# Staging the float64 words of the fourth weight matrix in two rooms of their own, in a delta-rule attention kernel with two feed-forward blocks

## The chip, the cores and the metric

The kernel runs on one core of one Trainium2 chip. The metric is the time of one execution on the device, in microseconds (us). In what follows PE is TensorE (the matmuls), DVE is VectorE, ACT is ScalarE, POOL is GpSimd and SP is the queue that issues the DMAs.

## What is computed

The reference is a delta-rule attention with a state per head, followed by two feed-forward blocks without a residual. The weights of the blocks come as float64, all else as float32.

```python
for t in range(S):                       # batch 4, 8 heads, S = 768, D = 48
    kt, vt, bt = (k_n[:, :, t], v[:, :, t], beta[:, :, t, None])
    y[:, :, t] = np.einsum('bhd,bhde->bhe', q[:, :, t], state)
    v_old = np.einsum('bhde,bhd->bhe', state, kt)
    state = state + bt[:, :, :, None] * np.einsum('bhd,bhe->bhde', kt, vt - v_old)
x = y.transpose(0, 2, 1, 3).reshape(3072, 384)
h = x @ w1_in;  x = np.maximum(0.01 * h, h) @ w1_out       # 384 -> 2048 -> 384
h = x @ w2_in;  out = (h - np.tanh(h)) @ w2_out            # 384 -> 2048 -> 384
```

## The kernel before

**Tiles.** The sequence is cut into 12 chunks n of 64 steps; two chunks make a unit u (6 units). A chunk carries 256 tokens (4 batches of 64 steps). For each unit the attention prepares keys and queries, Gram matrices, the inverse of a triangular matrix per head (`inverses(u)`, a chain of some sixty small POOL instructions), merges, states and outputs. `outputs(n)` writes the attention result of chunk n; it gathers its operands in two tiles of 128 partitions by 2048 float16, `Ub` and `Sb`, whose off-diagonal blocks must be zero. `to_xa(n)` scales and splits that result into the input of the first block; `to_xb(n)` does the same between the blocks.

**Feed-forward layers.** The last loop of the kernel calls `layer(n, i)` for each unit in the order (2u,0), (2u+1,0), (2u,1), (2u+1,1). A layer is 8 steps p. In each, `h_part` multiplies by the first matrix of block i (18 matmuls of 256 columns) and applies the nonlinearity, and three steps later (`LAG` is 3) `o_part` multiplies by the second matrix. All matmuls are made from float16 high and low halves.

**Weights.** The four matrices w1_in, w1_out, w2_in, w2_out are here called weights 0 to 3; each stands in 16 slices. `weights()` takes them one after the other. For each, `Weights.load` issues one DMA of 384 KB per slice, from float64 words into a *room* of 768 32-bit words per partition, as long as no room is asked for that still holds words not yet used. `convert` turns two slices at a time into float32 by three DVE instructions on the words (`w_f32`), sums their squares on ACT (the squares themselves are thrown away into the room), and then calls `load` again. Where the two rooms of a pair lie side by side in one tile the pair is one set of three instructions, 768 results wide; otherwise it is two sets of 384. After the eight pairs a matrix-wide scale is worked out (`sw`), and a second generator, `splits`, makes the float16 high half (two ACT instructions) and the low half (one on DVE or POOL) of each slice. `need((2 * i + 1, 2 * p + 1))` in `o_next` holds `o_part` back until the slices of its step are split.

The rooms of weights 3 are four of the eight slots of the tile that the matrix itself will fill (each used twice, for slices 0 to 7), and the first 768 words of `Ub` and of `Sb` (each used four times, for slices 8 to 15). So `weights()` waits for `("y", 1)`, the end of `outputs(1)`, before it touches weights 3, zeroes both tiles on POOL behind the conversion, and `outputs(n)` with n > 1 waits for `"w2"`, which stands for that.

**What sets the order.** The instructions are not ordered by hand. Every piece of work is a Python generator that yields the time from which it could go on, by a simple cost model kept in `Plan`. `Side.first` takes the generator with the smallest of that time plus a fixed delay for its kind (`d_...`); `Side.step`, called between matmuls of the layers, runs what is due; `Side.fill` puts pieces of `weights()` into gaps that the model sees on DVE; `need` and `layer` force work when the layers can't go on without it. The result is one fixed sequence per engine, and each engine runs its own in order. The delays and some other settings come from `START` until `"w2"` is done, then from `STEADY` (`tune`). Of the delays, smaller goes first: in `START` d_s2 is -1, d_w 0, d_s3 0.5, d_s1 1.0 and d_q (queries) 4.4; in `STEADY` d_q is 3.4, d_xa -1 in place of 0, and `step` is called after every second matmul of a layer, not every third.

Every instruction is issued in one helper, line 160, so the profile shows that line everywhere and the tiles tell what is what: `h_ps` and `o` are the sums of the layers, `a_ps` those of the attention and of the scales; `wo` and `wi` are weight tiles, `wst` the scaled slice, `wacc` the sums of squares; `X` and `Gd` the inverse; `sx`, `g`, `kap` and `osb` belong to the layers.

Of the kernel before, what the change touches and what calls it, by code (L numbers as in the profile page):

```python
# [7 lines left out]
F32 = mybir.dt.float32  # L8
# [183 lines left out]
def kernel(  # L192
# [13 lines left out]
    pe, act, dve, pool, sp = (Engine(plan, n) for n in ("pe", "act", "dve", "pool", "sp"))  # L206
# [8 lines left out]
    NF = w1_in.shape[1] // (KT * 128)  # L215
    DM = KT * 128
# [10 lines left out]
    def room(name, bufs, **kw):  # L227
        return Room(plan, ctx.enter_context(tc.tile_pool(name=name, bufs=bufs, **kw)), bufs)

    const, wts, live = (room(n, 1) for n in ("const", "wts", "live"))  # L230
# [16 lines left out]
    def copy(o, i, scale=1.0):  # L247
        act.activation(out=o, in_=i, func=ACTF.Copy, scale=scale)
# [16 lines left out]
    def cp(o, i, scale=None):  # L265

        op = "tensor_copy" if scale is None else "tensor_scalar"
        fa, fd = plan.finish("act", "activation", [i], [o]), plan.finish("dve", op, [i], [o])
        ca, cd = plan.cost("act", "activation", [o, i]), plan.cost("dve", op, [o, i])
        if fa + tune("cp") * (ca - cd) < fd:  # L270
            copy(o, i, 1.0 if scale is None else scale)
        elif scale is None:
            dve.tensor_copy(out=o, in_=i)
        else:
            dve.tensor_scalar(out=o, in0=i, scalar1=scale, scalar2=None, op0=ALU.mult)
# [74 lines left out]
    WO = [wts.tile([128, NF, 2, DM], F16, name=f"wo{i}") for i in range(2)]  # L350
    WI2 = [w.rearrange("p f c t n -> p f c (t n)") for w in WI]
    sw = const.tile([128, 6], F32, name="sw")

    def words(t):

        t = t.bitcast(I32)
        n = DM * 2
        return [t[:, i * n:(i + 1) * n] for i in range(t.shape[1] // n)]
# [64 lines left out]
    def weights():  # L423
        wi = [words(w.rearrange("p f c n -> p (f c n)")) for w in WI2]
        wo = [words(w.rearrange("p f c n -> p (f c n)")) for w in WO]
        nh = len(wi[0])

        x = [words(x_tile("w1"))[0] for _ in range(2)]
        a = Weights(0, w1_in, WI2[0], wo[0] + wo[1])
        b = Weights(1, w1_out, WO[0], ((wi[1] + x) * 2)[0:NF])  # L430
        yield Part([], 0)
        yield from a.convert()
        side.add(a.splits(), "s0")
        a = Weights(2, w2_in, WI2[1], (wo[1] * 2)[0:NF])
        yield from b.convert()
        side.add(b.splits(), "s1")
        done.add("w1")
        yield from a.convert()
        side.add(a.splits(), "s2")
        yield from wait(("y", 1))  # L440
        yield Part([], 0)
        bs = [words(t.rearrange("p c m n -> p (c m n)"))[0] for t in (Ub, Sb)]
        r = wo[1][nh // 2:] * 2 + bs * (NF // 4)
        b = Weights(3, w2_out, WO[1], r)
        yield from b.convert()
        for t in (Ub, Sb):
            pool.memset(t, 0.0)
        done.add("w2")
        side.add(b.splits(), "s3")

# [10 lines left out]
    Ub = live.tile([128, 2, GM, 128], F16, name="Ub")  # L461
    Sb = live.tile([128, 2, GM, 128], F16, name="Sb")
# [4 lines left out]
    def bank(n):  # L467
        t = ps_a.tile([128, 512], F32, tag="a", name="a_ps")
        return t[:, 0:GM * n].rearrange("p (m n) -> p m n", m=GM)

    def mm3(o, lb, ls, rhs, start=True, stop=True):
        mm(o, lb[:, 0, ls], rhs[0], start, False)
        mm(o, lb[:, 0, ls], rhs[1], False, False)
        mm(o, lb[:, 1, ls], rhs[0], False, stop)

    def halves(dst, src, n, w, rows=None):
        for h in range(2):
            r = (rows or HS)[h]
            cp(dst[r, :, :, w * h:w * h + n], src[r])
# [21 lines left out]
    def x_tile(owner):  # L501

        x_owner.append(owner)
        return x_p.tile([128, KT * N], F32, tag="x", name="x")
# [3 lines left out]
    def wait(key):  # L508
        if key not in done:
            yield lambda: key in done  # L510
# [371 lines left out]
    def outputs(n):  # L882
        u, s = n // 2, n % 2
        yield from wait(("u", n))
        yield from wait(("pp", n))
        yield from wait(("x", u))
        Q, P = q_t.pop(n), p_t.pop(n)
        if n > 1:
            yield from wait("w2")
            yield from wait(("r", n - 3))  # L890
            yield from wait(x_owner[-NX])
            x_t[n] = x_tile(("a", n))
        x32 = x_t[n].rearrange("p (t b i) -> p t b i", t=KT, b=B)

        def fill_y(g):
            halves(Ub, R[:, g], D, D)
            if n > 0:
                halves(Sb, SP[:, :, g * GM:(g + 1) * GM], D, D, HD)

        for g in range(NG):  # L900
            qs = qs_t[n, g]
            dve.tensor_scalar(out=qs[:, 4:5], in0=qs[:, 3:4], scalar1=sv_t[u, s][:, 3:4], scalar2=KS, op0=ALU.mult,
                              op1=ALU.mult)
        fill_y(0)
        for g in range(NG):
            yield Part([Ub, Sb, P[:, g]], 1)
            ps = bank(C)
            for m in range(GM):
                if n > 0:
                    mm3(ps[:, m], Sb, m, (Q[:, g, 0, m], Q[:, g, 1, m]), stop=False)  # L910
                mm3(ps[:, m], Ub, m, (P[:, g, 0, m], P[:, g, 1, m]), start=n == 0)
            if g + 1 < NG:
                fill_y(g + 1)
                done.add(("f", n))
            pv = ps.rearrange("p (b t) i -> p t b i", t=HP)
            xv = x32[:, :, g * 2:g * 2 + 2]
            sc = qs_t.pop((n, g))
            copy(xv[0:96], pv[0:96, 0:KT], sc[0:96, 4:5])
            for t_ in range(KT):
                cp(xv[96:128, t_], pv[32 * t_:32 * t_ + 32, KT], sc[32 * t_:32 * t_ + 32, 4:5])  # L920
        done.add(("y", n))
        side.add(to_xa(n), "xa")
# [25 lines left out]
    def to_xa(n):  # L948

        x = x_t.pop(n)  # L950
        yield max(plan.t["act"], at(x))
        sx = sm_p.tile([128, 4], F32, tag="sxs", name="sxs", bufs=4)
        pow2_scale(sx[:, 0:1], (yield from squares(x)), XT)
        yield at(sx[:, 0:1])
        xa_t[n] = x_split(x, sx[:, 0:1]), sx
        done.add(("n", n))
# [143 lines left out]
    def all_outputs():  # L1100
        for n in range(NS):
            yield from outputs(n)
# [60 lines left out]
    with tc.manual_schedule():  # L1163
# [18 lines left out]
        for gen, d in ((first_keys(), "k0"), (v_scale(0, 0), "v"), (all_outputs(), "o"), (all_states(), "s"),  # L1182
                       (all_products(), "p"), (all_merges(), "m"), (all_inverses(), "i"),
                       (all_grams(range(2)), "g0"), (all_queries(), "q"), (all_grams(range(2, 2 * NU)), "g"),
                       (all_keys(), "k")):
            side.add(gen, d)
        side.add(weights(), "w", True)
        plan.filler = side.fill
        for u in range(NU):
# [50 lines left out]
```

## Time and profile before

| | |
|---|---|
| median of 3 runs | 1244.53 us (1243.42 to 1246.35) |
| the profiled execution's own time | 1241.99 us |
| its span in the trace | 1240.3 us |
| PE busy in the span | 1012.0 us (82%) |
| DVE, ACT, POOL busy | 727.6, 635.0, 512.9 us |
| mean granted clock of PE | 0.959 of 2.4 GHz |

The durations below come from the profiled execution. Its time is 1.69 us above its span and 2.54 us below the median of the runs. Times of day in the text are us from the start of the span. A PE that is shown busy may still be running at the lower of its two clocks.

### The profile page before, as it was taken

To read this page: it belongs to the slowest core of one execution; us is meant where nothing else is said; L and a number is where in the kernel's file an instruction comes from. 1 tells how busy PE (TensorE), PEld (TensorE's weight loads), DVE (VectorE), ACT (ScalarE), POOL (GpSimd) and SP (SyncE) were. 2 spreads that over 40 slices of the span, in tenths; PEclk is the share of its full clock that TensorE was granted. 3 is DMA by queue.
4 is the path that set the end of the run, shared out by engine and by line. 5 is a ranking of instruction groups with operands and counts; after the bars stand their busy time and mean duration, and the time that the engine had idled before them with its cause. 6 is when DMAs were issued, how large, how long until landed. Compare 5 with 4: busy or idle time off the path is not lost.

```text
span 1240.3 us, 36912 instructions
## 1 busy us (share of the span) xinstructions
PE 1012.0 (82%) x16216; PEld 832.3 (67%) x16216; DVE 727.6 (59%) x1609; ACT 635.0 (51%) x1414; POOL 512.9 (41%) x635
## 2 busy tenths in 40 slices
PE   0202679682876999989998899979999999999998
PEld 0202568571765788867687786768867888778875
DVE  7998844886768756776566577326654154420243
ACT  3556687746475555745455655325543354333342
POOL 4697365398238624771177304831210221012100
PEclk9999999895788999989999999989999999999999
DMA  9423010421000101000101000001000000000001
GB/s 359 160 72 112 3 28 18 164 60 39 16 25 23 45 16 46 23 23 3 27 15 37 12 24 10 14 14 32 25 10 14 14 11 2 1 17 11 1 1 26
DMA packets 21857, 48.17 MB, mean 39 GB/s; under 512 B 4288, under 2 KB 7360, under 8 KB 21696
## 3 DMA queue, kind: packets, MB, share of 16 engines
q1 hardware_dynamic: 21696, 45.82, 11.8%
q8 instruction: 126, 2.06, 0.7%
q14 instruction: 35, 0.29, 0.1%
HBM read 41.09 MB, written 4.72 MB: 37 GB/s over the span
## 4 chain that ended last, share of the span: by engine, by line
PE 54%; DVE 22%; ACT 13%; POOL 6%; issue 4%; DMA 1%; SPq 0%; ACTq 0%; POOLq 0%; DVEq 0%
PE o L160 22%; PE h_ps L160 21%; PE a_ps L160 10%; POOL X L160 2%; DVE n L160 2%; DVE wi L160 2%; DVE wo L160 2%; DVE x L160 2%; DVE sx L160 2%; ACT g L160 2%; POOL Gd L160 2%; ACT junk L160 2%; DVE g L160 2%; ACT sx L160 1%; DVE Ub L160 1%
## 5 line engine op out<-in xcount | busy, mean ns | idle before, releaser
L160 PE MATMUL h_ps<-x,wi 128*128 128x256 f16 x3456 | 422.5, 275 | 18.7 <-DVE x L160 6.3
L160 PEld LDWEIGHTS <-wi 128*128 128x128 f16 x3456 | 334.2, 98 | 76.5 <-issue 15.8
L160 PE MATMUL o<-wo,g 128*128 128x384 f16 x1152 | 213.2, 334 | 22.3 <-ACT wo L160 7.4
L160 POOL TENSOR_TENSOR g<-sx,g 128x512 f16<-128x512 f32 x80 | 96.2, 1203 | 314.5 <-ACT g L160 305.3
L160 PE MATMUL o<-g,wo 128*128 128x256 f16 x1728 | 211.0, 275 | 0.0
L160 PEld LDWEIGHTS <-wo 128*128 128x128 f16 x1728 | 167.2, 98 | 31.5 <-issue 9.3
L160 ACT ACTIVATE g<-sx 128x512 f16<-128x512 f32 x192 | 121.0, 630 | 119.5 <-DVE sx L160 116.5
L160 PEld LDWEIGHTS <-g 128*128 128x128 f16 x1152 | 112.5, 99 | 88.1 <-issue 27.1
L160 DVE SCALAR_TENSOR_TENSOR sx<-sx,kap,h_ps 128x512 f32<-128x512 f32 x96 | 71.2, 742 | 98.5 <-ACT sx L160 98.3
L160 POOL TENSOR_TENSOR X<-X,Gd 128x30 f32<-128x30 f32 (+9 forms) x180 | 116.1, 645 | 14.1
L160 POOL TENSOR_TENSOR Gd<-X 128x30 f32<-128x30 f32 (+9 forms) x180 | 108.4, 602 | 27.6 <-DVE X L160 15.2
L160 ACT ACTIVATE sx<-h_ps,kap 128x512 f32<-128x512 f32 x96 | 65.5, 683 | 92.2 <-PE h_ps L160 86.5
L160 ACT ACTIVATE sx<-h_ps 128x512 f32<-128x512 f32 x96 | 56.6, 590 | 105.5 <-PE h_ps L160 101.5
L160 DVE SCALAR_TENSOR_TENSOR g<-sx,g 128x512 f16<-128x512 f32 x96 | 71.4, 743 | 64.7 <-ACT g L160 64.6
L160 PEld LDWEIGHTS <-KTp 64*64 64x64 f16 x3360 | 66.4, 119 | 36.0 <-issue 34.5
L160 PE MATMUL a_ps<-ab,ones 128*128 128x1 bf16 x124 | 11.4, 168 | 95.7 <-DVE ab L160 93.7
L160 POOL TENSOR_TENSOR P<-P,maskp 128x1024 f16<-128x1024 f16 x24 | 54.7, 2288 | 67.9 <-DVE P L160 66.4
L160 PEld LDWEIGHTS <-KN 64*64 64x64 f16 x1824 | 39.1, 123 | 43.4 <-issue 39.1
L160 PEld LDWEIGHTS <-ones 128*128 128x128 bf16 x124 | 7.7, 103 | 79.9 <-DVE ab L160 51.5
L160 DVE COPY Ub<-R 64x768 f16<-64x768 f16 x47 | 23.4, 498 | 56.6 <-PE a_ps L160 56.1
L160 PE MATMUL a_ps<-Q,KTp 64*64 64x64 f16 x1152 | 24.6, 199 | 23.3 <-ACT Q L160 20.2
L160 PE MATMUL a_ps<-Q,Sb 128*128 128x64 f16 x528 | 36.7, 201 | 8.4 <-DVE Sb L160 8.4
(165 smaller groups left out, 1538.8 us busy)
## 6 DMA issues: line engine op xcount, KB each, us to landing
wo<-in_w_in_dram SPq DMA_DIRECT2D x32, 384.0 KB, 6.5
qf<-in_q_dram SPq DMA_DIRECT2D x24, 256.0 KB, 3.1
wi<-in_w_out_dram SPq DMA_DIRECT2D x14, 384.0 KB, 7.8
kf<-in_k_dram SPq DMA_DIRECT2D x12, 384.0 KB, 3.8
vf<-in_v_dram SPq DMA_DIRECT2D x12, 384.0 KB, 3.6
out_dram<-osb SPq DMA_DIRECT2D x48, 96.0 KB, 2.2
wo<-in_w_out_dram SPq DMA_DIRECT2D x8, 384.0 KB, 5.4
Ub<-in_w_out_dram SPq DMA_DIRECT2D x4, 384.0 KB, 3.3
```

The source lines that it names most:

```text
L160: return getattr(self.eng[eng], op)(*args, **kw)
```

## The change

The two rooms that lay in `Ub` and `Sb` become two rooms in a new tile of 128 partitions by 1536 32-bit words, `stage`. The waits on `("y", 1)` and on `"w2"` go, and so do the two memsets behind the conversion. The four other rooms, the number of DMAs and the order of the four matrices stay.

```diff
     sw = const.tile([128, 6], F32, name="sw")
+    stage = wts.tile([128, 2 * DM * 2], F32, name="stage")
...
         side.add(a.splits(), "s2")
-        yield from wait(("y", 1))
-        yield Part([], 0)
-        bs = [words(t.rearrange("p c m n -> p (c m n)"))[0] for t in (Ub, Sb)]
-        r = wo[1][nh // 2:] * 2 + bs * (NF // 4)
+        r = (wo[1][nh // 2:] * 2)[0:NF // 2] + words(stage) * (NF // 4)
         b = Weights(3, w2_out, WO[1], r)
         yield from b.convert()
-        for t in (Ub, Sb):
-            pool.memset(t, 0.0)
         done.add("w2")
         side.add(b.splits(), "s3")
...
         if n > 1:
-            yield from wait("w2")
             yield from wait(("r", n - 3))
```

## Rows read from the trace of the kernel before

**Rows 1.** Windows of the span: busy us (instructions) per engine, PE clock, DMA.

```profile
224.70:275.20 50.50, 47.26 (x621) 40.29 (x622) 42.47 (x83) 31.05 (x87) 34.59 (x42) 0.97 0.34 106
275.20:301.60 26.40, 0.73 (x19) 0.61 (x17) 19.60 (x44) 11.86 (x42) 21.91 (x35) 0.58 0.15 45
301.60:420.00 118.40, 96.30 (x1946) 74.81 (x1946) 83.38 (x187) 69.21 (x165) 64.55 (x90) 0.85 0.09 26
```

**Rows 2.** Timeline of PE: start, duration, instruction, [idle before <- releaser].

```profile
273.08 2.12 PE L160 MATMUL h_ps<-x,wi 128*128 128x256 f16 x18 [0.74 <-DVE sx L160]
290.58 0.16 PE L160 MATMUL a_ps<-ab,ones 128*128 128x1 bf16 x1 [15.38 <-DVE ab L160]
299.01 0.56 PE L160 MATMUL a_ps<-ab,ones 128*128 128x1 bf16 x16 [8.27 <-DVE ab L160]
301.60 4.00 PE L160 MATMUL o<-wo,g 128*128 128x384 f16 x12 [2.02 <-ACT wo L160]
307.89 2.11 PE L160 MATMUL o<-wo,g 128*128 128x384 f16 x12
```

**Rows 3.** Waits of PE from 301.7 to 420: for whom, total us, times, longest.

```profile
PE o L160 <- ACT wo L160: 7.4, 3, 2.8
PE o L160 <- ACT osb L160: 5.7, 1, 5.7
PE o L160 <- DVE wo L160: 1.9, 1, 1.9
```

**Rows 4.** Timeline of SP, loads of weights 3: the first eight of sixteen.

```profile
219.32 1.85 SPq L160 DMA_DIRECT2D wo<-in_w_out_dram  x4
232.68 6.46 SPq L160 DMA_DIRECT2D wo<-in_w_out_dram  x4
```

**Rows 5.** Timeline of DVE: scale of weights 2, two conversions of weights 3.

```profile
144.34 0.17 DVE L160 RECIPROCAL sw<-p 128x1 f32<-128x1 f32 x1
227.36 0.96 DVE L160 SCALAR_TENSOR_TENSOR wo<-wo 128x768 int32<-128x768 int32 x1
232.45 0.56 DVE L160 TENSOR_SCALAR wo<-wo 128x768 int32<-128x768 int32 x1
```

**Rows 6.** Timeline of ACT: sum of squares, and one split, of weights 3.

```profile
231.72 0.84 ACT L160 ACTIVATE wo<-wo 128x768 bf16<-128x768 f32 x1 [0.58 <-DVE wo L160]
232.47 0.19 ACT L160 ACTIVATION_READ_ACCUMULATOR wo<-wo 128x1 f32 x1
302.05 0.60 ACT L160 ACTIVATE wst<-wo,sw 128x384 f32<-128x384 f32 x1
302.68 0.52 ACT L160 ACTIVATE wo<-wst 128x384 f16<-128x384 f32 x1
```

**Rows 7.** Windows behind the scale of weights 2: columns as in Rows 1.

```profile
144.00:160.00 16.00, 10.47 (x309) 9.74 (x306) 13.95 (x37) 13.16 (x27) 7.05 (x7) 1.00 0.02 5
160.00:204.00 44.00, 38.39 (x621) 33.86 (x618) 16.85 (x47) 41.56 (x105) 31.42 (x31) 1.00 0.11 31
204.00:224.70 20.70, 10.80 (x234) 9.30 (x231) 15.64 (x53) 10.59 (x24) 3.60 (x4) 0.83 0.24 77
```

**Rows 8.** Tile wo: all conversions of one kind: min/median/max ns.

```profile
L160 DVE SCALAR_TENSOR_TENSOR wo<-wo x8: 925/1105/1868, 227.4 to 250.1; 128x768 int32<-128x768 int32 x8
```

**Rows 9.** Timeline of POOL: one memset of the two.

```profile
301.61 1.81 POOL L160 MEMSET Ub<- 128x2048 f16 x1
```

**Rows 10.** Timelines: inputs of chunks 2, 3 ready (DVE); layers (2,0), (3,0) begin (PE).

```profile
377.32 0.36 DVE L160 COPY x<-xhi 128x768 f16<-128x768 f16 x1
432.08 1.20 DVE L160 COPY x<-xhi 128x768 f16<-128x768 f16 x1
420.04 2.13 PE L160 MATMUL h_ps<-x,wi 128*128 128x256 f16 x18
479.59 1.04 PE L160 MATMUL h_ps<-x,wi 128*128 128x256 f16 x8
```

**Rows 11.** Timeline of PE: layer (1,0) begins.

```profile
224.73 0.82 PE L160 MATMUL h_ps<-x,wi 128*128 128x256 f16 x3 [4.40 <-DVE ab L160]
```

## The prediction

> **What bounds the kernel now.** I read the windows first, to see whether PE is full in each stretch. From 224.7 to 275.2 it is busy for 47.26 of 50.5 us; then, for the 26.4 us up to 301.6, for 0.73; and from 301.6 to 420 for 96.30 of 118.4, at a mean granted clock of 0.85 [rows 1]. So there is one hole, and behind it a stretch that is neither full nor at full clock. The timeline of PE shows what stands behind the hole: the last layer matmuls end at 275.20; two small sums of squares follow after 15.38 and 8.27 us; then, 2.02 us after the second, come the first matmuls of 384 columns that read `wo`, released by ACT's split of it [rows 2]. The releaser named for the first two waits is only that of the tiny matmul that happened to be next in PE's fixed order. What the layers lack is weights 3: the 16 matmuls at 299.01 are the sum for their scale, and the layer goes on with the first split slice. The waits of PE name the same thing afterwards, in small: 7.4 us for ACT's `wo` (2.02 of it the row at 301.60) and 1.9 for DVE's [rows 3]; there the splits of weights 3 arrive one by one, beside the layer that uses them.
>
> Then I asked why weights 3 are late. Their first load is issued at 219.32 [rows 4], though the scale of weights 2, the last thing ahead of them in `weights()`, was worked out at 144.34 [rows 5]. The 75 us between are the wait for `outputs(1)`, which owns `Ub` and `Sb`. That wait is what the change takes away.
>
> **The parts of the change, step by step.**
>
> A. *The hole.* Weights 3 took from 219.32 to the sum at 299.01, 79.7 us, in a stretch shared with everything else. At that same pace a start at 144.3 ends at 224, some 50 us ahead of 275.20. So all three waits go: 15.38 + 8.27 + 2.02 = 25.7 us [rows 2].
>
> B. *The splits beside the layer.* With the scale known by 224 the 16 slices are split before the layer begins on them. 7.4 - 2.02 + 1.9 = 7.3 us go [rows 3]. The 5.7 us for ACT's `osb` stand in the same list; I leave them, as nothing ties them to the weights.
>
> C. *The clock.* After the hole 12 matmuls take 4.00 us; the next such 12 take 2.11 [rows 2]: the lower level (1.2 GHz) after PE had stood still, then the higher. 1.9 us go for certain. The bound on the other side is the whole stretch: 0.85 on 118.4 us means 17.8 us lost to the clock [rows 1], idle time included. I take 6, nearer to the lower end, because part of that stretch follows waits that stay.
>
> D. *What weights 3 now lie beside.* This is the term that the trace of before can't show, because the work moves. On DVE it is eight sets of one instruction of 0.56 and two of 0.96 us [rows 5], 19.8 us; the four pairs of narrow sets become wide ones, since both rooms of `stage` lie in one tile, which makes 24 instructions of 36. DVE is busy for 13.95 of 16 us up to 160, but for 16.85 of 44 up to 204 [rows 7]: 27 us are free there. ACT is the narrow place: eight sums of squares of 0.84 + 0.19, or 8.2 us, and 16 splits of 0.60 + 0.52, or 17.9 us [rows 6]. ACT is busy for 41.56 of 44 us from 160 to 204 and for 10.59 of the next 20.7 [rows 7]. It carries the splits of weights 1 and 2 there, the nonlinearity of layer (0,0), and the queries that `outputs(1)` needs. `outputs(1)` sets the start of layer (1,0), for which PE stands and waits at 224.73 [rows 11]. So each us by which ACT is late there can move the whole chain. Lower bound: PE is idle for 9.9 of the last 20.7 us [rows 7], and since the settings of `STEADY`, which come earlier now, put the queries a little further forward, up to 9.9 could even be won. Upper bound: 8.2 + 17.9 = 26.1 us lost, if all of it is put ahead of `outputs(1)` and none falls into idle time. The squares have a smaller delay than the queries and fall where ACT is 94% busy, so I count their 8.2 in full; the splits can start only when all is converted, near 200 by the free time on DVE, and ACT has some 10 us free behind that: I count 0.8. Together 9.
>
> E. *What costs nothing here.* The 16 loads move ahead of loads of q, k and v on SP, and a load that waits for its room holds those behind it: four issues took 6.46 us once [rows 4]. The q load for `outputs(1)` is behind some of them; up to 6 us are inside the bounds of D. The two memsets, 2 x 1.81 us [rows 9], leave POOL's chain for the inverse of unit 1; that only makes the input of chunk 2 earlier. The wait for `"w2"` in `outputs(n)` ended near 300, before chunk 2's outputs could have run, so its removal changes nothing. If the cover of this part is gone, that is, if chunk 2's input becomes the late thing, the 3.6 us begin to count.
>
> F. *What is late next.* The input of chunk 2 is ready at 377.68 and layer (2,0) begins at 420.04: 42.4 us of room; for chunk 3, 433.28 against 479.59: 46.3 us [rows 10]. A gain of up to 42 us therefore reaches layer (2,0) undiminished even if the attention is not a us earlier, and behind it PE is close to full.
>
> The sum: -25.7 - 7.3 - 6 + 9 = -30.0. The span of 1240.3 becomes 1210.3, the execution's own time 1212.0; the median of the runs lies 2.5 above that, which gives 1214.5 us.
>
> **The rivals.** *More is won.* D costs nothing and most of the clock comes back: 25.7 + 7.3 + 17.8 = 50.8, but F caps that at 42.4, and with the 3.6 of the memsets at 46: 1198.5. For it speaks that ACT is idle for 15.4 us between 144 and 224.7 [rows 7], against it that most of this idle time lies behind 204.
>
> *ACT gives it back.* All 26.1 us of D fall ahead of `outputs(1)`: -39 + 26.1 = -12.9, or 1231.6. For it: ACT at 94%, and the delay of s3 (0.5) is smaller than that of s1 (1.0), whose slices layer (0,0) waits for.
>
> *POOL and DVE hold each other up.* The same conversion of 768 words took 925 ns at least, 1868 at most [rows 8]. If each of the 16 long conversions, in their new place, holds up one of POOL's low halves for layer (0,0) by its 0.95 us, 15.2 us come on top of D: -14.8, or 1229.7. POOL is busy for 31.42 of the 44 us there [rows 7], but it is not what PE waits for. The Trainium skill, SBUF — State Buffer, section "SBUF: two separate sides", speaks against the change here: a DVE instruction with two inputs from SBUF and a POOL instruction that reads SBUF exclude each other for a whole instruction. By that rule this rival would be the rule; the spread of the row agrees with it, but not with a full instruction lost each time, since the median is 1105.
>
> *Slower.* The conversions are put in front of layer (0,0)'s input as well. DVE has 2.05 us free from 144 to 160 [rows 7]; if all 19.8 us are put there, chunk 0's input comes 17.7 us later, and with the 26.1 on ACT that makes 43.8 against the 39.0 of A, B and C: 4.8 us slower, 1249.3. It decides from the point where layer (1,0) begins 39 us after 224.73. Against it: a piece of the weights is put in only where the planner sees a gap or nothing more urgent.
>
> *It doesn't do what it says.* Weights 3 stay as late as they are, because the planner serves them last: 1244.5. For that, their 79.7 us would have to become 157.
>
> **How the numbers follow.** Forecast 0.57, more won 0.15, ACT gives it back 0.12, POOL and DVE 0.05, no change 0.03, slower 0.08. The first four are faster by over 0.2% (2.5 us, about what a measurement of this kernel can tell from no change): 0.89; within it 0.03; slower 0.08. The range takes in the forecast with D at either of its ends near the value taken (1202 to 1226), reaches down to the cap of F and up to the rival on ACT: 1198 to 1232; it leaves out the last two cases and the edges of the others.
>
> **What would show it.** A: no wait of PE above some 5 us between 225 and 320, and the 16 matmuls of the scale before 225. B: no waits of layer (0,1) for `wo`. C: a granted clock above 0.9 up to the start of layer (2,0). D: the start of layer (1,0), forecast at 234, between 215 and 251; ACT nearly full to 215. F: layer (2,0) begins near 390, with its input ready before that; if PE stands still in front of it, F was the wrong bound. The forecast is wrong if layer (1,0) begins after 250, or if the 30 us are there at 420 and gone at the end, in new waits of the late layers for `x` or `osb`.

## The result and the profile after

The changed kernel took 1222.09 us, the median of runs between 1221.22 and 1225.41, against 1243.97 us (1241.15 to 1246.35) for the kernel before beside it: a ratio of 0.983, 95% interval 0.9802 to 0.9858. That is 21.9 us less; 30.0 less were forecast, and the range of 1198 to 1232 holds the time. The profiled execution took 1222.18 us, with a span of 1220.3 us, a PE busy for 1013.1 us (83%) and a mean granted clock of 0.97.

First the windows of the changed kernel, in the stretches of [rows 1] and the first two of [rows 7]; the columns are those of [rows 1].

```profile
224.70:275.20 50.50, 45.14 (x622) 38.67 (x620) 30.17 (x88) 42.79 (x109) 32.33 (x40) 0.97 0.12 36
275.20:301.60 26.40, 22.80 (x170) 17.02 (x169) 20.37 (x37) 13.25 (x29) 22.55 (x33) 0.94 0.00 1
...
144.00:160.00 16.00, 8.05 (x221) 7.55 (x218) 15.22 (x38) 11.78 (x24) 6.53 (x7) 1.00 0.05 9
160.00:204.00 44.00, 32.01 (x592) 27.38 (x592) 34.91 (x62) 38.44 (x89) 25.29 (x26) 1.00 0.33 113
```

In the 26.4 us in which PE had worked for 0.73, it now works for 22.80. From 160 to 204 DVE goes from 16.85 to 34.91 us: there the conversions of weights 3 now lie. PE works less there than before, 32.01 us against 38.39.

The same in PE's timeline, at the first matmuls of 384 columns, with the ACT instruction that they waited for in front, and the waits of PE between 301.7 us and the start of layer (2,0); these answer to [rows 2] and [rows 3].

```profile
284.76 0.85 ACT L160 ACTIVATE x<-o 128x512 f32<-128x512 f32 x2
285.39 3.22 PE L160 MATMUL o<-wo,g 128*128 128x384 f16 x12 [3.13 <-ACT x L160]
```

```profile
PE o L160 <- ACT osb L160: 4.1, 1, 4.1
PE h_ps L160 <- DVE x L160: 1.3, 1, 1.3
...
```

The hole of 25.7 us has become one wait of 3.13, for ACT to read out the sums `o` of the layer before (`x<-o`), and not for weights; no wait for `wo` is left, and the three waits left out of the list are of 1.0, 0.3 and 0.2 us.

To see where the gain goes from there, I cut both spans at the starts of the same layers on PE: (0,0), (1,0), (2,0), (4,0) and (6,0). Windows of the kernel before:

```profile
0.00:171.07 171.07, 48.81 (x1542) 45.43 (x1542) 141.98 (x257) 97.94 (x222) 107.06 (x131) 1.00 0.38 133
171.07:224.73 53.66, 40.91 (x583) 35.42 (x582) 25.95 (x85) 41.40 (x105) 27.11 (x26) 0.93 0.13 41
224.73:420.04 195.31, 144.33 (x2584) 115.70 (x2585) 145.41 (x312) 112.12 (x293) 121.05 (x165) 0.84 0.16 49
420.04:616.50 196.46, 183.66 (x3569) 149.57 (x3567) 131.00 (x313) 107.60 (x270) 84.32 (x105) 0.96 0.08 23
616.50:793.20 176.70, 165.96 (x2894) 136.29 (x2893) 112.22 (x256) 95.75 (x224) 94.03 (x131) 0.99 0.07 20
793.20:1240.30 447.10, 428.36 (x5052) 349.93 (x5050) 171.05 (x389) 180.21 (x307) 79.31 (x78) 0.99 0.05 12
```

And of the changed kernel:

```profile
0.00:181.70 181.70, 49.33 (x1542) 46.05 (x1543) 157.42 (x277) 103.81 (x235) 110.63 (x133) 1.00 0.42 147
181.70:235.00 53.30, 43.81 (x598) 37.13 (x598) 40.65 (x89) 42.54 (x104) 25.61 (x23) 0.97 0.24 75
235.00:381.40 146.40, 133.82 (x2313) 107.14 (x2313) 92.34 (x214) 88.37 (x217) 71.39 (x98) 0.93 0.07 19
381.40:567.10 185.70, 168.97 (x2985) 139.20 (x2985) 131.53 (x287) 103.26 (x260) 115.46 (x160) 0.94 0.09 24
567.10:770.10 203.00, 184.60 (x3569) 149.95 (x3567) 130.17 (x307) 112.17 (x280) 84.03 (x104) 0.95 0.08 23
770.10:1220.30 450.20, 432.54 (x5217) 352.32 (x5211) 184.41 (x421) 183.83 (x316) 101.97 (x118) 0.99 0.05 12
```

The first two columns are the whole account. A window's length less PE's busy time is PE's idle time:

| stretch, up to the start of | idle before | idle after | difference | busy, difference |
|---|---|---|---|---|
| (0,0) | 122.3 | 132.4 | +10.1 | +0.5 |
| (1,0) | 12.8 | 9.5 | -3.3 | +2.9 |
| (2,0) | 51.0 | 12.6 | -38.4 | -10.5 |
| (4,0) | 12.8 | 16.7 | +3.9 | -14.7 |
| (6,0) | 10.7 | 18.4 | +7.7 | +18.6 |
| the end | 18.7 | 17.7 | -1.1 | +4.2 |
| sum | 228.3 | 207.2 | -21.1 | +1.0 |

Read from top to bottom: layer (0,0) begins 10.6 us later, (1,0) still 10.3 later, (2,0) 38.6 earlier. That is 38.4 us less idle time and 10.5 us less work between (1,0) and (2,0), against the late start of 10.3. Of these 38.6 the end sees 20.0 of the span. Two things take the rest behind (2,0): 10.5 us more of idle time, and 8.1 us more of work. That work is no more in all; the changed kernel has 2313 matmuls between (1,0) and (2,0) where the kernel before had 2584, and does the others later.

### The profile page after: what moved, and what is told of

It is laid out like the page before. It is cut to its first block, busy times and chain, and to the rows that moved or that the text cites. A ratio compares the mean times of both kernels' runs of the same rounds, so it can differ in the third digit from the quotient of the medians.

```text
span 1220.3 us, 36850 instructions
## 1 busy us (share of the span) xinstructions
PE 1013.1 (83%) x16216; PEld 831.8 (68%) x16216; DVE 736.5 (60%) x1592; ACT 634.0 (52%) x1409; POOL 509.1 (42%) x635
## 4 chain that ended last, share of the span: by engine, by line
PE 51%; DVE 26%; ACT 11%; POOL 8%; issue 4%; DMA 0%; ACTq 0%; SPq 0%; DVEq 0%; POOLq 0%
PE o L160 21%; PE h_ps L160 19%; PE a_ps L160 11%; DVE n L160 4%; POOL X L160 3%; POOL Gd L160 3%; DVE x L160 2%; ACT g L160 2%; DVE wi L160 2%; DVE g L160 2%; DVE sx L160 2%; DVE wo L160 2%; ACT junk L160 1%; ACT sx L160 1%; DVE X L160 1%
## 5 line engine op out<-in xcount | busy, mean ns | idle before, releaser
L160 PE MATMUL h_ps<-x,wi 128*128 128x256 f16 x3456 | 427.9, 276 | 18.3 <-DVE x L160 12.3
L160 POOL TENSOR_TENSOR g<-sx,g 128x512 f16<-128x512 f32 x78 | 93.1, 1194 | 311.6 <-ACT g L160 291.6
L160 PEld LDWEIGHTS <-wo 128*128 128x128 f16 x1728 | 167.4, 98 | 32.3 <-issue 10.5
L160 DVE SCALAR_TENSOR_TENSOR g<-sx,g 128x512 f16<-128x512 f32 x96 | 74.3, 774 | 67.4 <-ACT g L160 67.4
L160 POOL TENSOR_TENSOR P<-P,maskp 128x1024 f16<-128x1024 f16 x24 | 52.6, 2196 | 61.4 <-DVE P L160 58.2
L160 ACT ACTIVATE x<-a_ps,qs 32x128 f32<-32x128 f32 (+1 forms) x57 | 25.5, 447 | 31.4 <-PE a_ps L160 28.2
```

The costliest lines, as they stand in the source:

```text
L160: return getattr(self.eng[eng], op)(*args, **kw)
```

## Experiments

**The wait or the rooms?** The kernel `e2_rooms_only` has everything of the change but keeps the wait for `outputs(1)`.

```diff
+        yield from wait(("y", 1))
+        yield Part([], 0)
         b = Weights(3, w2_out, WO[1], r)
```

> The two rooms of their own and the wide conversions, without the memsets, but weights 3 again wait for the end of chunk 1's outputs. Theory (the wait makes the gain, the rooms by themselves nothing): layer (0,0) begins at 171, layer (1,0) at 225, the hole before the first matmuls of layer (0,1) is there again with 15 to 26 us, and the time is 1238 to 1245. Rival (fewer and wider conversions and the missing memsets make a good part of the gain): the hole is under 10 us and the time 1222 to 1235.

Measured: 1246.29 us, ratio 1.0034 (1.0018 to 1.0051). PE's timeline, as [rows 2]:

```profile
289.08 0.16 PE L160 MATMUL a_ps<-ab,ones 128*128 128x1 bf16 x1 [15.05 <-DVE ab L160]
296.76 0.57 PE L160 MATMUL a_ps<-ab,ones 128*128 128x1 bf16 x16 [7.51 <-DVE ab L160]
299.35 0.80 PE L160 MATMUL o<-wo,g 128*128 128x384 f16 x2 [2.02 <-ACT wo L160]
```

The hole is back, within 1.1 us of its size (24.6 against 25.7). The time is 1.3 us above the 1238 to 1245 of the theory, and far from the rival's. New rooms, wide conversions and the missing memsets show no gain by themselves; the hole comes with the wait.

**Do the conversions ahead of chunk 0 cost anything?** In the changed kernel layer (0,0) waits for the input of chunk 0 on DVE, with conversions of weights 3 ahead of it (DVE's timeline, the first of them and the end of the input, then PE's):

```profile
146.52 0.66 DVE L160 TENSOR_SCALAR wo<-wo 128x768 int32<-128x768 int32 x1
...
180.70 0.95 DVE L160 COPY x<-xhi 128x768 f16<-128x768 f16 x1
```

```profile
181.70 1.65 PE L160 MATMUL h_ps<-x,wi 128*128 128x256 f16 x7 [5.57 <-DVE x L160]
```

Between 144 and 181.6 DVE spends 14.5 us on weights 3. `e1_wait_n0` lets `weights()` begin them only when that input is written.

```diff
+        yield from wait(("n", 0))
+        yield Part([], 0)
         b = Weights(3, w2_out, WO[1], r)
```

> The changed kernel, but the loads and conversions of weights 3 begin only when the input of chunk 0 has been made (in the changed kernel they begin behind the scale of weights 2). Theory: the 10.6 us by which layer (0,0) begins late (181.7 against 171.1) are conversions of weights 3 that DVE does ahead of chunk 0's input. Then layer (0,0) begins at 171 +- 2 again, layer (1,0) between 225 and 230, and, weights 3 being ready well before 285, the time falls by 5 to 10 us below the changed kernel, to 1212 to 1217. Rival, as it stood in the prediction (ACT is the narrow place): layer (0,0) begins at 171, but the sums of squares then all fall ahead of chunk 1's output, layer (1,0) still begins at 233 or later, and the time stays at 1219 to 1225. Third possibility: the layers are set by the attention from layer (2,0) on, whose input is ready at 381; then the start is earlier and the end is not.

Measured: 1220.01 us, ratio 0.9827 (0.9812 to 0.9842). The starts of layers (0,0) and (1,0) in PE's timeline:

```profile
171.39 1.89 PE L160 MATMUL h_ps<-x,wi 128*128 128x256 f16 x8
234.58 0.80 PE L160 MATMUL h_ps<-x,wi 128*128 128x256 f16 x3 [1.63 <-DVE x L160]
```

So the conversions did delay (0,0), and it is back to 0.3 us of its old place; but (1,0) stays at 234.58 and the time where it was. The theory had (1,0) before 230 and 1212 to 1217; all three numbers are those of the rival, and the third possibility, an earlier start without an earlier end, fits too. The conversions and sums of squares now lie between (0,0) and (1,0), where PE is idle for 18.9 us against 9.5; whether DVE or, as the rival says, ACT holds chunk 1 up there was not separated.

**Wide or narrow conversions?** `e4_two_tiles` makes the two rooms separate tiles, so that the conversions are narrow again, as they were.

```diff
-    stage = wts.tile([128, 2 * DM * 2], F32, name="stage")
+    stage = [wts.tile([128, DM * 2], F32, name=f"stage{i}") for i in range(2)]
...
-        r = (wo[1][nh // 2:] * 2)[0:NF // 2] + words(stage) * (NF // 4)
+        r = (wo[1][nh // 2:] * 2)[0:NF // 2] + [words(t)[0] for t in stage] * (NF // 4)
```

> The changed kernel with the two rooms in two tiles, so that the last four pairs are converted by two narrow sets each (36 instructions on DVE in place of 24). By the durations of the kernel before that is some 2 us more on DVE and 1.6 us more on ACT, ahead of the hole's place, where nothing waits for it. Theory: layer (1,0) begins at 235 to 238 and the time is 1219 to 1226. Rival (the width matters): more than 1228.

Measured: 1228.7 us, ratio 0.9902 (0.9883 to 0.9921). The hole is gone (6.1 us idle in the 30 us ahead of the first matmul of 384 columns, against 3.1 in the changed kernel and 26.4 before). The 6.6 us lost come late: (2,0) begins at 380.0, a little earlier than in the changed kernel, and (6,0) at 787.0 instead of 770.1. Layer (1,0), at 235.1, came where the theory had it, the time in the range of the rival (more than 1228). Whether the 6.6 us belong to narrow conversions or to another order of everything else is what the next runs ask.

**How much is one order worth?** Any edit changes the model's times, and with them the order of the rest. I changed one constant of the planner, `GAP`, the pause that its model puts between an instruction and one on another engine that reads its result, in the changed kernel (`p_a`) and in the kernel before (`p_b`).

```diff
-GAP = 0.15
+GAP = 0.16
```

> The changed kernel, with one constant of the planner's cost model moved from 0.15 to 0.16: the same instructions in a slightly other order. Theory A (the 11 us that are lost again behind layer (2,0) come from what is computed and from its limits): the time stays within 3 us of the changed kernel, 1219 to 1225, with idle time of PE behind 420 between 40 and 47 us. Theory B (they are an accident of the order that the planner happens to draw): the time moves by 4 to 10 us one way or the other.

> The kernel before with the planner's constant at 0.16 in place of 0.15. The changed kernel with the same edit took 1240.7 us in place of 1222.1, so an order can be worth 18 us. Theory A (the order matters only where the layers follow close behind the attention, as in the changed kernel; in the kernel before the hole keeps them apart): the time stays within 4 us of the kernel before, 1238 to 1247. Theory B (any new order moves the time by that much, in either kernel): it differs from the kernel before by 6 to 20 us. Either way the hole in front of layer (0,1)'s second matmuls is there, 18 to 28 us.

And with 0.14:

> The changed kernel with the constant at 0.14: a third order of it, beside 0.15 (1222.1 us) and 0.16 (1240.7). If the order is worth some 10 us at random, 1218 to 1242; the hole is not there (under 8 us), and layer (1,0) begins between 230 and 240 in all three. The mean over three orders of this kernel less that over three orders of the kernel before is what the change is worth apart from the order: 15 to 25 us by the theory (hole and slow splits gone, 10 us given back at the start), 0 to 10 if most of the 22 us was luck.

> The kernel before with the constant at 0.14: a second order of the same work. Theory A: 1238 to 1247. Theory B: 6 to 20 us away from the kernel before. The hole is there, 18 to 28 us.

| GAP | before, us (ratio, interval) | changed, us (ratio, interval) | difference |
|---|---|---|---|
| 0.14 | 1253.93 (1.0114, 1.0082 to 1.0146) | 1244.37 (1.003, 1.0014 to 1.0046) | -9.6 |
| 0.15 | 1243.97 | 1222.09 (0.983, 0.9802 to 0.9858) | -21.9 |
| 0.16 | 1258.74 (1.0144, 1.0115 to 1.0172) | 1240.66 (1.0006, 0.9988 to 1.0025) | -18.1 |

The ratios are to runs of the kernel before with 0.15 made beside each kernel; its medians there were 1243.97, 1241.54 and 1240.0 us. For the changed kernel with 0.16 neither theory had room: 18.6 us are more than the 10 of theory B, and with 0.14 it is above the 1242 named. For the kernel before theory B held. The changed kernel is the faster in all three rows, by 16.5 us on average, but a hundredth in one constant moves either kernel by 10 to 22 us. So the size can't be read from one pair, and not even the sign: the changed kernel with 0.14 is not faster than the kernel before with 0.15. What speaks for the sign is all the orders together: the four with the wait (the three here and `e2_rooms_only`) took 1243.97 to 1258.74, the eight without it in this document that compute everything 1215.9 to 1244.37. The 6.6 us of `e4_two_tiles` mean nothing by themselves. What can be read in all orders is a thing that comes with the wait each time. In the 30 us ahead of the first matmul of 384 columns the kernels with the wait are idle for 26.4, 24.6, 19.7 and 19.1 us (before, `e2_rooms_only`, 0.14, 0.16); the changed kernel, its two neighbours, `e1_wait_n0` and `e4_two_tiles` for 3.1, 5.1, 4.3, 7.0 and 6.1.

**Do the settings of STEADY come too early?** They begin with `"w2"`, which follows the conversions of weights 3, and these now end soon after 218.8, where before the memsets behind them ran at 301.61 [rows 9]. `e3_steady_late` holds the settings back until layer (0,1) has been issued.

```diff
-        return (STEADY if "w2" in done else START)[name]
+        return (STEADY if "w2" in done and ("b", 0) in done else START)[name]
```

> The changed kernel, but the settings of STEADY come into use only once layer (0,1) has issued its first matmuls to the end (near 303), about where they came in the kernel before (near 300), and not at 229. Theory (the earlier switch of settings has no part in the gain): no hole, layer (1,0) at 232 to 238, layer (2,0) at 375 to 400, the time 1215 to 1240, within the spread of orders. Rival (the earlier settings make the gain): layer (2,0) after 405 and more than 1240.

Measured: 1233.69 us, ratio 0.9944 (0.9921 to 0.9968); (1,0) at 235.5, (2,0) at 385.9, all as the theory had it. That speaks against the settings as a cause of the give-back, but 11.6 us are within what an order is worth: inconclusive on size.

**Is it the inverse that holds layer (2,0)?** In the changed kernel (2,0) begins in the moment in which its input is there. DVE's last instruction for that input and PE's first with it:

```profile
381.04 0.36 DVE L160 COPY x<-xhi 128x768 f16<-128x768 f16 x1
381.45 1.57 PE L160 MATMUL h_ps<-x,wi 128*128 128x256 f16 x8 [1.28 <-DVE x L160]
```

In [rows 10] 42.4 us lay between the two. The chain of waits of the changed kernel goes through the inverse of unit 1 on POOL up to 314 and from there mostly over PE. `h_a_half_inverse` (changed kernel) and `h_b_half_inverse` (kernel before) leave out every second substitution step of the inverse, about half of its POOL instructions, so this part of the computation is not done there.

```diff
-            if lo < hi:
+            if lo < hi and j % 2:
```

> The changed kernel without every second step of the substitution that inverts the triangular matrices (about 30 of some 60 POOL instructions per unit are left out, some 25 us of POOL per unit). Theory (with the hole closed, the layers have caught up with the attention, and the chain through the inverse on POOL is what they wait for next): layer (2,0) begins at 355 to 372 in place of 381, the idle time of PE between the starts of (2,0) and (6,0) falls from 35 us to under 27, and the time to 1195 to 1212. Rival (behind 381 PE waits for the layers' own steps on ACT and DVE, not for the inverse): layer (2,0) moves by less than 8 us or the idle time behind it stays at 33 to 45, and the time stays at 1214 to 1240.

> The kernel before with the same steps of the inverse left out. Theory (there the hole bounds layer (0,1) and the attention has 42 us to spare): the hole stays at 18 to 28 us, layer (2,0) begins within 8 us of 420, and the time stays within 8 us of the kernel before, 1233 to 1249. Rival (the attention bounds this kernel too, or the shorter POOL chain frees DVE for weights 3): the time falls by more than 12 us.

Measured: 1203.6 us, ratio 0.9676 (0.9635 to 0.9718), for the changed kernel, and 1225.04 us, ratio 0.9856 (0.9821 to 0.9891), for the kernel before. Both fall by 18 to 19 us. In the changed one the input is now early (DVE's timeline, then PE's):

```profile
352.11 0.36 DVE L160 COPY x<-xhi 128x768 f16<-128x768 f16 x1
362.37 0.82 PE L160 MATMUL h_ps<-x,wi 128*128 128x256 f16 x6
```

Layer (2,0) begins 19.1 us sooner and no longer waits for it. Not all of this is the inverse of unit 1: that of unit 0 is shorter too, and (0,0) begins 17.4 and (1,0) 6.1 us sooner. But PE is still idle for 32.4 us between (2,0) and (6,0), where the theory had said less than 27: a shorter inverse does not take the idle time behind (2,0) away. And the kernel before, with nothing else changed, lost over half of its hole (PE's timeline: one wait of 11.29 is left), which the theory had held impossible:

```profile
285.84 0.56 PE L160 MATMUL a_ps<-ab,ones 128*128 128x1 bf16 x16 [11.29 <-DVE ab L160]
```

The rival, that the inverse takes part in the hole too, held: weights 3 start behind `outputs(1)`, and with the shorter inverse their first load is issued at 190.28 in place of 219.32 [rows 4].

**Can the give-back be had?** The two lists of PE's waits between layers (2,0) and (6,0) (for whom, total us, times, longest). Before:

```profile
...
PE o L160 <- ACT osb L160: 0.9, 2, 0.5
```

After:

```profile
PE o L160 <- ACT osb L160: 11.4, 3, 5.9
PE a_ps L160 <- DVE ab L160: 7.4, 4, 5.5
```

What is new stands at the top: ACT's scaling of a finished output, `osb`, which frees the sums that the next layer writes to. One of these waits in DVE's, ACT's and PE's timelines:

```profile
538.14 2.40 DVE L160 SCALAR_TENSOR_TENSOR g<-sx,g 128x512 f16<-128x512 f32 x1 [0.70 <-ACT g L160]
540.46 0.14 DVE L160 TENSOR_SCALAR kap<-sw 128x1 f32<-128x1 f32 x1
```

```profile
541.08 0.58 ACT L160 ACTIVATE osb<-o,kap 128x384 f32<-128x384 f32 x1 [2.98 <-DVE kap L160]
```

```profile
541.71 1.76 PE L160 MATMUL o<-wo,g 128*128 128x384 f16 x5 [5.18 <-ACT osb L160]
```

The factor `kap` is made by three short DVE instructions (the first, of 0.14 us, is shown), which stand in DVE's queue behind one of 2.40; ACT waits for them, and PE waits for ACT. The factor needs only scales known when the layer begins. `e5_scale_early` moves `out_scale(kap)` from the end of the layer to its start.

```diff
         kap = kappa(sx)
+        need((3, "s"))
+        out_scale(kap)
```

> The changed kernel with one step moved: the factor by which a finished layer (n,1) is scaled (three DVE instructions of one column) is worked out at the layer's start, when the scale of weights 3 has long been known, and not at its end. Theory: the waits of PE for ACT's osb (19.5 us in the changed kernel from 160 on, 10 to 16 in the kernel before) come from that factor, which stands on DVE behind the low halves of the layer's last step; moved, they fall under 8 us. If the order of the rest were the same the time would fall by some 10 us, to 1212; the orders tried so far of this kernel spread over 1222 to 1244, so the waits are the test and the time is not: 1205 to 1235. Rival (the two accumulators are drained late because ACT and DVE are behind anyway): the waits for osb stay at 13 us or more.

Measured: 1215.9 us, ratio 0.9798 (0.9766 to 0.9829). Over the whole of 160 us to the end the waits for `osb` fall from 19.6 to 2.9 us:

```profile
PE a_ps L160 <- DVE ab L160: 11.3, 6, 3.2
PE h_ps L160 <- DVE sx L160: 10.9, 4, 5.6
PE o L160 <- ACT osb L160: 2.9, 2, 2.6
```

In the changed kernel `ab` stood at 9.2 and `sx` at 2.9: they rose where `osb` fell, and the idle time from (2,0) to PE's last matmul is 47.0 us against 47.4. The 6.2 us that it won lie ahead of (2,0), which begins at 374.0. Of the kernels that compute everything it is the fastest, below both the changed one and the one before; the gain over the changed kernel is within what an order is worth.

**And without the delay of (0,0)?** `e6_new_delays` adds to that other delays in `START` and `STEADY`: weights and their last splits go later, queries and values sooner.

Of the two lines of settings only the entries that change are shown, with the values of `START` before:

```diff
-'lag': 4.0, 'd_v': 1, 'd_s3': 0.5, 'd_p': 0, 'd_q': 4.4, 'd_w': 0
+'lag': 4.5, 'd_v': 0.5, 'd_s3': 3, 'd_p': 0.25, 'd_q': 2.4, 'd_w': 1
```

> The kernel of the run before this one with other delays in START and STEADY (queries 2.4, splits of weights 3 at 3, conversions of weights at 1, values 0.5, products 0.25, lag 4.5): queries go ahead of the splits and the conversions. If the start is held up by conversions and splits ahead of chunk 0's input and of the queries, layer (0,0) begins at 171 to 176 and layer (1,0) before 232, no hole comes back (under 8 us), and the time is 1195 to 1215. If the order of the rest decides, it is anywhere from 1215 to 1240.

Measured: 1220.61 us, ratio 0.9821 (0.9797 to 0.9844). PE's timeline at the starts of (1,0) and (2,0):

```profile
222.30 0.80 PE L160 MATMUL h_ps<-x,wi 128*128 128x256 f16 x3 [6.31 <-DVE x L160]
377.09 0.58 PE L160 MATMUL h_ps<-x,wi 128*128 128x256 f16 x2 [2.75 <-DVE x L160]
```

In `STEADY` d_q goes from 3.4 to 2.4; all else is as shown. The whole delay is gone: (1,0) begins 12.7 us sooner than in the changed kernel and (0,0), at 160.8, 20.9 sooner. At (2,0) 4.4 of that are left, and at the end 1.5. Against `e5_scale_early`, from which it differs by the delays alone, (2,0) is 3.1 us later and the time 4.7 us longer. So the time is not the 1195 to 1215 of an earlier start, but in the range named for the case that the order of the rest decides.

## Why the prediction was right, and where not

**A, the hole: right.** Its place, its size (25.7 us) and its cause held. `e2_rooms_only` brings it back by the wait alone, and it is small in each order without the wait. The 16 matmuls of the scale ran at 225.96, a microsecond after the 225 named as a sign.

**B, the splits beside the layer: right.** The waits for `wo` of [rows 3] are gone, and those for ACT's `osb` in the same list stay, 4.1 us for 5.7.

**C, the clock: this term was mis-sized.** 6 us were counted; about 1 came. Taken along the granted clock, from the first clock entry of each trace (at 169.9 and 187.2 us) to the end, PE was busy at the lower of its two levels for 63.6 us in the kernel before and is for 61.4 in the changed one, and PE's whole busy time went from 1012.0 to 1013.1. The 12 matmuls at 301.60 no longer take 4.00 us, as [rows 2] had it, but their successors take 3.22 at 285.39, and a new stretch at the lower clock lies from 327.2 to 340.8. PE's timeline:

```profile
326.05 0.65 PE L160 MATMUL o<-wo,g 128*128 128x384 f16 x3 [4.15 <-ACT osb L160]
...
331.32 2.74 PE L160 MATMUL a_ps<-X,AT 64*64 64x32 f16 x96
```

At the higher level 96 of the same small matmuls take 1.90 (PE's timeline of the kernel before):

```profile
431.35 1.90 PE L160 MATMUL a_ps<-X,AT 64*64 64x32 f16 x96
```
The forecast "above 0.9 up to (2,0)" held as a number (0.93 in the window from 235 to 381.4), and yet won next to nothing. The step that failed is the one that gave a share of the lost clock in [rows 1] to the hole: it fell with waits which the change only moves.

**D, what weights 3 lie beside: right in size, wrong in place, and its price at the end not shown.** 9 us were counted at (1,0); it begins 10.3 us later, at 235.0 for a forecast 234. But in the changed kernel the delay isn't ACT's. It stood already at (0,0), where it was 10.6 us, behind 14.5 us of conversions on DVE, put ahead of chunk 0's input. That is the mechanism of the rival "slower": DVE was full from 144 to 160 (15.22 of 16 us) as that rival had it, and 10.6 of its 17.7 us came. The reason given against it, that pieces of weights go only where the planner sees a gap or nothing more urgent, did not hold. What it cost at the end can't be told: in `e1_wait_n0` and `e6_new_delays` the delay of (0,0) goes, in the second that of (1,0) too, and the time moves by 2.1 and 1.5 us, far less than an order is worth. And where `e1_wait_n0` takes DVE's part away, (1,0) is as late as with it, as the prediction's reasoning on ACT would have it.

**E, what costs nothing: right in that no cost of it was seen, wrong in its one claim.** The memsets leaving POOL were to make chunk 2's input earlier. It came 3.7 us later, at 381.40 for the 377.68 of [rows 10]. The inverse of unit 1 began at 261.45 on POOL, for 250.27 before, three times the 3.6 us of the memsets. That this made chunk 2's input late is not shown: in `e1_wait_n0` the same inverse began at 252.31, and the input still came at 382.90.

**F, what is late next: half right, and this is the step whose second half failed.** The bound was right: chunk 2's input was the next late thing, and (2,0) came 38.6 us earlier, 4 short of the cap of 42.4. The start was forecast near 390; it was 381.45. "With its input ready before that" was wrong. In the changed kernel and in the seven other orders without the hole and with the whole inverse, (2,0) begins within 0.1 us of its input, whatever the time of that is:

```profile
397.32 0.36 DVE L160 COPY x<-xhi 128x768 f16<-128x768 f16 x1
397.74 1.65 PE L160 MATMUL h_ps<-x,wi 128*128 128x256 f16 x7 [1.44 <-DVE x L160]
```

(the changed kernel with `GAP` 0.16; the first line is DVE's, the second PE's). And "behind it PE is close to full" was read from the kernel before, where it was true, and I now read the hole itself as the reason: in those 26 us POOL worked for 21.91 and DVE for 19.60 [rows 1], and the attention got ahead of the layers. With the hole gone that lead is gone. The first instruction of the inverse of unit 2, which layer (4,0) will need, in POOL's timeline, before and then after:

```profile
367.23 0.25 POOL L160 TENSOR_TENSOR Gd<-X 128x30 f32<-128x30 f32 x1 [2.03 <-DVE X L160]
```

```profile
394.78 0.41 POOL L160 TENSOR_TENSOR Gd<-X 128x30 f32<-128x30 f32 x1 [1.06 <-DVE X L160]
```

Before, it began 52.8 us ahead of layer (2,0); after, 13.3 us behind it. In the four orders with the wait it began 52.8 to 69.9 us ahead, in the eight without it between 5.7 ahead and 18.1 behind. PE is idle between (2,0) and (6,0) for 23.5, 23.9, 28.8 and 29.3 us in the four orders with the wait and the whole inverse, and for 35.1 to 49.2 us in the eight without it. Each of these eight is above each of those four, so this isn't the accident of one order. It is the other half of the failure that the prediction named: gained at 420, given back in new waits of the late layers. That the one makes the other is argued and not shown. Layer (3,0) still begins within 0.1 us of its input in six of the eight orders, but (4,0) and (6,0) do not wait for theirs: these are at least 16 us early in all eight, in the changed kernel 30.3 us (DVE's timeline, then PE's) and 56.6 us. What PE waits for behind (2,0) are other instructions of the layers and the attention on ACT and DVE.

```profile
536.10 0.69 DVE L160 COPY x<-xhi 128x768 f16<-128x768 f16 x1
567.12 1.14 PE L160 MATMUL h_ps<-x,wi 128*128 128x256 f16 x9
```

**The sum.** From A, B, C and D -30 was forecast at (2,0) and at the end. At (2,0) it was -38.6: A and B came in whole, 5.4 us of other waits went too, 10.5 us of work were put off until later, and the late start took 10.3. At the end 18.6 of them had been given back, 8.1 as that work and 10.5 as idle time. The forecast was 7.6 us too low, by one term that was left out (the idle time that comes back behind (2,0)) and one of a wrong size (C). That the time fell into the range is in part the luck of the order: with `GAP` at 0.14 and 0.16 the changed kernel took 1244.37 and 1240.66, above the 1232, though the kernel before was slower there too. And the 1202 to 1226 given for D's ends follow from no D of the text: its bounds of -9.9 and 26.1 give 1195.6 and 1231.6.

**The rivals.** *ACT gives it back* is out: 1231.6 was to come of ACT ahead of `outputs(1)`, and ACT was not what was late in the changed kernel. *POOL and DVE*: the conversion with two inputs took 895 to 1658 ns from `wo` and 945 to 2876 from `stage`, at a median of 1168 and 1555 (1105 before, [rows 8]). In the timeline of tile `wo`:

```profile
L160 DVE SCALAR_TENSOR_TENSOR wo<-wo x8: 895/1168/1658, 151.0 to 176.0; 128x768 int32<-128x768 int32 x8
L160 DVE SCALAR_TENSOR_TENSOR wo<-stage,wo x8: 945/1555/2876, 178.8 to 218.8; 128x768 int32<-128x768 int32 x8
```

They took longer than before, most of all the second eight; in sum the sixteen took 22.4 us, 7.3 more than at 0.945 each. The longest of them stands in DVE's timeline over a POOL instruction that began 0.30 us before it (DVE, then POOL):

```profile
204.01 2.88 DVE L160 SCALAR_TENSOR_TENSOR wo<-stage,wo 128x768 int32<-128x768 int32 x1
```

```profile
203.71 2.37 POOL L160 TENSOR_TENSOR P<-P,maskp 128x1024 f16<-128x1024 f16 x1 [2.16 <-DVE P L160]
```

POOL's ended at 206.08 and DVE's 0.81 us behind that, about the 0.945 of one that nothing holds up. The rule of the Trainium skill cited in the prediction (SBUF — State Buffer, section "SBUF: two separate sides") agrees with this pair. The mechanism is there in this pair, then. How much of the 7.3 us it makes, and what share they have in the late start, no run separates; the 15.2 us of this rival did not come. *More is won* stopped at the cap of F, and the rest went to the give-back.

**What stays open.** That the lost lead makes the new idle time is read from orders only, not from an edit that gives the lead back: a shorter inverse moves (2,0) but leaves 32.4 us of idle time behind it, and `e5_scale_early` takes one kind of wait away and others fill its place. What sets the pace there, DVE's queue or the alternation of PE and DVE, was not settled.

## What to carry to other kernels

A hole on the bounding engine is not lost to the others: look at what POOL and DVE do in it, and ask where that work will lie without it, before you count the hole as gain to the end. Where a program orders the instructions, run the kernel before and the changed one in two or three neighbouring orders, and believe what all orders have in common; one pair gives neither the size nor, by itself, the sign. Where a clock is low behind a hole, look for the other waits in that stretch before you credit the clock to the hole.

## What the runs showed that was not expected

PE ran at the lower clock for 13.7 us, from 327.2 to 340.8, while it was busy all the time, behind a wait of 4.15 us. The mean granted clocks of two runs can't simply be compared: executions of the changed kernel at 0.97 and at 0.911 took 1222.18 and 1221.99 us, at spans of 1220.3 us both. The window up to (0,0) shows 1.00 in the changed kernel and 0.63 in `e1_wait_n0`, but PE ran at the same speed in both (PE's timeline of the changed kernel, then of `e1_wait_n0`, where the clock of this stretch is 0.50):

```profile
120.83 5.30 PE L160 MATMUL a_ps<-X,AT 64*64 64x32 f16 x192 [1.12 <-DVE X L160]
```

```profile
120.87 5.30 PE L160 MATMUL a_ps<-X,AT 64*64 64x32 f16 x192 [1.16 <-DVE X L160]
```

Both are at the lower level: at the higher one 96 of these matmuls took 1.90 us, so 192 would take about 3.8. The trace of the changed kernel has no clock entry ahead of 187.2 us, that of the kernel before none ahead of 169.9, and the 1.00 shown for such a stretch, in [rows 7] up to 169.9 too, is no measured clock. And one constant of the planner, changed by a hundredth, moved this kernel by as much as the change under study.
